# Gated linear attention and a SoLU block: v and state in 64 columns, and query products dealt out among the wide ones

## The chip, the cores and the metric

The kernel runs on one core of a Trainium2 chip. A core has a matrix engine (TensorE, PE in the profile; its weight loads are PEld), three engines for elementwise work (VectorE or DVE, ScalarE or ACT, GpSimd or POOL) and SyncE (SP), which issues most transfers. Each engine works through its own queue in order, and semaphores hold an instruction until what it needs is there. Products are written to PSUM, eight banks of 512 float32 columns on 128 partitions. The metric is device time in microseconds; the kernel before has a median of 407.49 over 14 runs (402.58 to 410.55).

## The reference

Attention with a decaying state for 4 batches, 8 heads, 768 tokens and 48 dimensions per head, then a feed-forward block on 3072 tokens (384 to 1024 to 384):

```python
for t in range(S):
    state = alpha[:, :, t, :, None] * state + np.einsum('bhd,bhe->bhde', k[:, :, t], v[:, :, t])
    y[:, :, t] = np.einsum('bhd,bhde->bhe', q[:, :, t], state)
# x = y as (tokens, heads * dims)
h = x @ w_in
e = np.exp(h - h_max)
solu = h * e / (sum(e) + 1e-09)
ln = (solu - mean(solu)) / sqrt(var(solu) + 1e-06) * g_ln
return ln @ w_out
```

All inputs and outputs are float32.

## The kernel before

Tokens are taken in six groups of 128 per batch; a group holds all four batches. Within a group attention is written as matrix products: running products of alpha scale queries and keys (`scan_back`, `scan_on`, `queries`, `keys`), `scores` multiplies keys with queries, `masked` keeps the causal half as `sT`, and the output `y` of a batch is the sum of two kinds of products, both made by `y_mm` (L298) into one PSUM bank per batch:

- `read_state` (L315): queries times the state left by the earlier groups. A head's 48 dimensions are split into 32 and 16. The 32 of head h lie in row h of `qv` and `state`; the 16 of two heads share a row of 32 partitions, and `qv` rows 8 to 15 hold that row once for each head, with the other head's half set to zero by `parity` (`apart`, L235). A product has 32 rows by 32 columns of weights and 128 tokens, so 16 of them have places of their own in the 128x128 array (four batches by four column places `r`). There are four parts: `parts` 0 and 1 give the first 32 output dimensions of heads 0 to 3 and 4 to 7, parts 2 and 3 the last 16 of the even and of the odd heads. Each part has 2 x 4 x 4 = 32 products, 128 in all.
- `read_values` (L323): `sT` times v, 64 products with all 128 rows and 32 columns of weights. Then ScalarE copies each batch's bank to `x`.

`next_state` (L333) makes keys times v: 32 products with 64 columns for the heads' first 32 key dimensions, 16 with 128 columns (two heads side by side) for the shared rows; VectorE adds the two banks to `state` (L351; in group 0 ScalarE copies them). `decay` (L246), on GpSimd, multiplies the state by the group's whole decay before it is read. `keys_back` (L284) turns the keys back with 12 transposes for `next_state`.

In `vn` and `state` a head has 80 columns: dimensions 0 to 31 in columns 0 to 31, dimensions 32 to 47 in 48 to 63, zeros elsewhere. `last` picks 32 columns that hold the 16 and 16 zeros, so the 16 of an even and of an odd head land on different halves of 32 output rows.

The feed-forward block has two wide products: `up_mm` (L362), three of 512 columns into `h`, and `down` (L471), four of 385 columns into `o` for each half. The program is written under a manual schedule: the order of calls is the order on each engine. For each group g the loop from L858 has eight steps s. A step makes `up(g, s)`, attention work of group g + 1, and half a `down` of group g - 1. Three tables, `first` (g = 1), `second` (g = 2) and `usual`, say which attention work stands at the head of a step, behind `up`, in the middle (ahead of `down`) and in the tail. So attention of group 2 stands in `first`, of group 3 in `second`, of groups 4 and 5 in `usual`; groups 0 and 1 stand in an opening written by hand (L651 to L783). In the steps that the change touches, `usual` has scores in the tails of steps 4 and 5, the masks at the heads of 5 and 6, query products of parts 0 and 1 in the tail of step 6, parts 2 and 3 in the middle of step 7, values and the next state in its tail. No group follows group 5.

The other queues that the change passes: SyncE issues the loads in the order of the program (`load_v`, two transfers a group, ahead of the loads of k and q of the next group), and GpSimd has the decay between running sums (L397) and the small `pow` instructions of `finish` (L508).

Of the kernel before, what the change touches and what calls it, by code (L numbers as in the profile page):

```python
# [9 lines left out]
FP = mybir.dt.float32  # L10
# [4 lines left out]
ALU = mybir.AluOpType  # L15
AX = mybir.AxisListType
P = 128
# [15 lines left out]
def fast_path(ctx, tc, q, k, v, alpha, moe_w_in, moe_w_out, moe_g_ln, out):  # L33
# [12 lines left out]
    nc = tc.nc  # L46
    B, H, S, D = q.shape
# [4 lines left out]
    NP = H // 2  # L52
    NB = H + NP
    E0, E1 = 32, 16
    KC = DM // P
    FC = DFF // P
    HF = FC // 2
# [7 lines left out]
    const = pool("const", 1)  # L65
# [37 lines left out]

    VW = 80
    vn = const.tile([P, B, H, VW], FP, name="vn")
    state = const.tile([P, 2 * H, VW], FP, name="state")
    last = [slice(48, 80), slice(32, 64)]
    SW = P + 1  # L110
    aT = const.tile([P, NB, SW], FP, name="aT")
    seed = [const.tile([P, NP, SW], FP, name=f"seed{i}") for i in range(2)]
# [53 lines left out]

    def load_v(g):
        t = slice(g * P, (g + 1) * P)
        for dst, src in ((slice(0, E0), slice(0, E0)), (slice(48, 64), slice(E0, D))):
            nc.sync.dma_start(  # L170
                out=vn[:, :, :, dst].rearrange("p b h d -> p (b h) d"),
                in_=v[:, :, t, src].rearrange("b h p d -> p (b h) d"),
            )

    def load_v_first(slot):
        x = slots[slot].rearrange("p (n d) -> p n d", d=D)
        y = vn.rearrange("p b h d -> p (b h) d")
        nc.sync.dma_start(out=x, in_=v[:, :, 0:P].rearrange("b h p d -> p (b h) d"))
        for dst, src in ((slice(0, E0), slice(0, E0)), (slice(48, 64), slice(E0, D))):
            nc.gpsimd.tensor_copy(out=y[:, :, dst], in_=x[:, :, src])  # L180


    def firsts(src, dst):
# [62 lines left out]
    def decay(g):  # L246

        if g == 0:
            return
        s = state[:, 0:H, 0:64]  # L250
        nc.gpsimd.tensor_tensor(out=s, in0=s, in1=h4[:, 0:H, 1:2].to_broadcast([P, H, 64]), op=ALU.mult)
        for i in range(2):
            s = state[:, H : 2 * H, 0:64].rearrange("p (j i) e -> p j i e", i=2)[:, :, i]
            nc.gpsimd.tensor_tensor(out=s, in0=s, in1=h4[:, H:NB, 1:2].to_broadcast([P, NP, 64]), op=ALU.mult)

    def quarter(b):
        return slice(32 * b, 32 * b + 32)

    def banks(name, shape, n=B):
        return [ps_a.tile([P] + shape, FP, tag=f"a{b}", name=f"{name}{b}") for b in range(n)]  # L260
# [30 lines left out]

    parts = [(a, [(NP * a + r, slice(0, E0)) for r in range(NP)]) for a in range(2)]
    parts += [(2, [(2 * r + i, last[i]) for r in range(NP)]) for i in range(2)]
    reading = {}

    def y_mm(b, a, r, row, lhsT, rhs, stop=False):  # L298
        begun = reading["begun"]
        nc.tensor.matmul(  # L300
            y_bank(b)[quarter(r), a], lhsT=lhsT, rhs=rhs, start=(b, r) not in begun, stop=stop,
            tile_position=(row, 32 * r), skip_group_check=True,
        )
        begun.add((b, r))

    def read_begin():
        reading["y"] = {}
        reading["begun"] = set()

    def y_bank(b):  # L310
        if b not in reading["y"]:
# [2 lines left out]

    def read_state(n):  # L315
        a, hs = parts[n]
        for rows in (0, H):
            for r, (h, e) in enumerate(hs):
                for b in range(B):
                    p = quarter(b)  # L320
                    y_mm(b, a, r, 32 * b, state[p, rows + h, e], qv[p, rows + h])

    def read_values(g, batches=range(B)):  # L323
        if 0 in batches:
            gr[g]["x"] = pair.tile([P, KC, B, P], FP, name="x")
        for b in batches:
            for n, (a, hs) in enumerate(parts):
                for r, (h, e) in enumerate(hs):
                    y_mm(b, a, r, 0, vn[:, b, h, e], sT[:, b, h], n == len(parts) - 1)
        for b in batches:  # L330
            nc.scalar.copy(out=gr[g]["x"][:, :, b], in_=reading["y"][b])  # L331

    def next_state(g):  # L333
        kv = banks("kv", [H, 64], 2)
        for j in range(NB):
            for b in range(B):
                if j < H:
                    o, e = kv[0][quarter(b), j], vn[:, b, j, 0:64]
                else:
                    i = 2 * (j - H)  # L340
                    o, e = kv[1][quarter(b), i : i + 2], vn[:, b, i : i + 2, 0:64]
                nc.tensor.matmul(  # L342
                    o, lhsT=kg[:, j, quarter(b)], rhs=e, start=True, stop=True, tile_position=(0, 32 * b),
                    skip_group_check=True,
                )
        for i in range(2):
            s = state[:, H * i : H * i + H, 0:64]
            if g == 0:
                nc.scalar.copy(out=s, in_=kv[i])
            else:  # L350
                nc.vector.tensor_tensor(out=s, in0=s, in1=kv[i], op=ALU.add)  # L351

# [7 lines left out]
    def up_mm(g, f):  # L362
        d = gr[g]
        h = ps_h.tile([P, T4], FP, tag="h", name="h")
        for a in range(KC):
            nc.tensor.matmul(  # L366
                h, lhsT=w_in[:, a, f * P : (f + 1) * P], rhs=d["x"][:, a].rearrange("p b t -> p (b t)"),
                start=(a == 0), stop=(a == KC - 1),
            )
        d["h"] = h  # L370

    def up_act(g, f):
# [95 lines left out]
        d["r"] = small.tile([P, B], FP, name="r4")  # L468
        nc.gpsimd.tensor_tensor(out=d["r"], in0=s[:, :, 3], in1=mhalf.to_broadcast([P, B]), op=ALU.pow)

    def down(n, half):  # L471
        g, b = divmod(n, B)
        d = st[n]
        if half == 0:
            d["o"] = ps_o.tile([P, 512], FP, tag="o", name="o")
        for f in range(half * HF, half * HF + HF):
            nc.tensor.matmul(  # L477
                d["o"][:, 0 : DM + 1], lhsT=u_of(g, f)[:, b * P : b * P + P], rhs=w_out[:, f], start=(f == 0),
                stop=(f == FC - 1), skip_group_check=True,
            )  # L480

    def finish(n):
        g, b = divmod(n, B)
# [143 lines left out]
    nc.scalar.dma_start(out=g_rows, in_=moe_g_ln.rearrange("(c p) -> c p", p=P))  # L627
    load_first(k, kn, 0)
    load_first(q, qn, 0)
    nc.gpsimd.memset(vn, 0.0)  # L630
    nc.gpsimd.memset(unit, 0.0)
    nc.gpsimd.memset(unit[:, :, 0:1], 1.0)
    nc.gpsimd.memset(aT[:, :, 0:1], 0.0)
# [42 lines left out]
    scores(0, 0)  # L676
    t = [x.tile([P, NP, P], FP, tag=n, name="a_" + n) for x, n in ((ps_h, "h"), (ps_o, "o")) for _ in range(2)]
    scores(0, 1, t)
    read_begin()
    masked(0)  # L680
    masked(1)
    bits(0)
# [7 lines left out]
    for f in range(FC):  # L690
        p = 2 + f // 2
# [75 lines left out]
    masked(1)  # L767
    finish(2)
    alpha_T(2)
    down(3, 0)  # L770
    read_begin()
    read_state(0)
    read_state(1)
    down(3, 1)
    read_state(2)
    read_state(3)
    alpha_over(2)
    load(alpha, an, 3)
    for i in range(3):
# [7 lines left out]
    usual = dict(  # L787
        head={4: "keys_back", 5: "masked0", 6: "masked1"},
        behind={0: "v keys", 1: "on2 on0 on1", 2: "lasts firsts", 3: "apart", 5: "decay", 6: "alpha", 7: "back"},
        tail={4: "scores0", 5: "scores1", 6: "begin read0 read1", 7: "values"},  # L790
        middle={7: "read2 read3"},
    )
    first = dict(
        head={4: "keys_back", 6: "masked0", 7: "masked1"},
        behind={0: "v keys", 1: "on2 on0", 2: "on1 lasts", 3: "firsts", 4: "apart", 5: "decay", 7: "alpha"},
        tail={5: "scores0", 6: "scores1", 7: "begin read0 read1 read2 read3 values"},
        middle={},
    )
    second = dict(
        head={4: "keys_back", 6: "masked0", 7: "masked1"},  # L800
        behind={0: "back_late", 1: "v keys", 2: "on2 on0 on1", 3: "lasts firsts", 4: "apart", 5: "decay", 6: "alpha", 7: "back"},
        tail={5: "scores0", 6: "scores1", 7: "read2 read3 values"},
        middle={7: "begin read0 read1"},
    )

    def attend(a, what):

        more = a + 1 < G
        if what == "v":
            load_v(a)  # L810
        elif what == "keys":
            keys_T(a)
            keys(a)
            if more:
                load(k, kn, a + 1)
        elif what[:2] == "on":
            scan_on(a, int(what[2]))
        elif what == "lasts":
            lasts(qn, qe)
            queries(2)  # L820
        elif what == "firsts":
            firsts(qn, qv[:, 0:H])
            queries(0)
            queries(1)
            if more:
                load(q, qn, a + 1)
        elif what == "apart":
            apart()
        elif what == "decay":
            decay(a)  # L830
        elif what == "keys_back":
            keys_back(a)
        elif what[:6] == "scores":
            scores(a, int(what[6]))
        elif what[:6] == "masked":
            masked(int(what[6]))
        elif what == "alpha" and more:
            alpha_T(a + 1)
            alpha_over(a + 1)
            if a + 2 < G:  # L840
                load(alpha, an, a + 2)
        elif what == "back" and more:
            for i in range(3):
                scan_back(a + 1, i)
        elif what == "back_late":
            for i in range(3):
                scan_back(a, i)
        elif what == "begin":
            read_begin()
        elif what[:4] == "read":  # L850
            read_state(int(what[4]))
        elif what == "values":
            read_values(a)
            next_state(a)

    centres = {4: (0, 1), 6: (2, 3), 7: (4, 5, 6, 7)}
    todo = []
# [528 lines left out]
```

## Time and profile before

| what | value |
|---|---|
| median of the runs | 407.49 us |
| the profiled execution | 403.4 us |
| its span, first to last instruction | 401.6 us |
| granted TensorE clock | 0.994 |
| TensorE products, busy | 375.2 us |
| VectorE busy | 255.8 us |
| ScalarE busy | 146.3 us |
| GpSimd busy | 117.6 us |
| `h`, 288 passes | 133.9 us |
| `o`, 384 passes | 133.2 us |
| queries with state, 1280 passes | 20.1 us |
| `sT` with v, 768 passes | 22.9 us |
| keys with v, 384 and 192 passes | 7.0 and 6.5 us |

A float32 product leaves two records on TensorE, called passes here; a transpose leaves one. In a row of the timeline the columns are the start and length in us, the engine, the line, the operation, output and inputs by name, the tile of the array (rows * columns of weights), the shape of the moving operand, the count, and in brackets the idle time before it with what ended it. Products overlap, so a group's busy time is the union of its records, and the step from one row's start to the next is what the row cost.

### The profile page before, as it was taken

The numbers are of one execution on the slowest core, as the hardware profiler recorded it, in microseconds if no ns is written. First come the engines' busy times: TensorE is split into PE (matmuls) and PEld (weight loads), VectorE is DVE, ScalarE is ACT, GpSimd is POOL, SyncE is SP. The second block draws the span as 40 slices with busy tenths as digits, with TensorE's granted clock in tenths as the row PEclk, the third lists the DMA queues.
The fourth block names the chain that finished last, engine by engine and source line by source line (L and its number), as shares of the span: only waits on it lengthen the run. The fifth ranks groups of instructions, "written<-read, shape, count | busy, mean of one in ns | idle before, by whom it ended". The sixth has DMA issues, their size and how long they took to land. (4 is left out here: it accounts for less than half of the span.)

```text
span 401.6 us, 11119 instructions
## 1 busy us (share of the span) xinstructions
PE 375.2 (93%) x4929; PEld 227.8 (57%) x4929; DVE 255.8 (64%) x415; ACT 146.3 (36%) x253; POOL 117.6 (29%) x118
## 2 busy tenths in 40 slices
PE   8686999779897998999999999999999999999995
PEld 8673355446653467555657555666556575555552
DVE  0979779996649883798691894674875413444510
ACT  3636674553432534223443143243152132233100
POOL 5010000030005894076510446210475110333200
PEclk9999999999999899999999999999999999999999
DMA  9966989304327304543040932003300000000011
GB/s 183 197 162 181 223 258 155 81 20 99 101 52 128 80 4 95 67 100 78 22 101 11 155 81 54 2 23 61 40 20 21 23 3 21 20 20 12 30 41 47
DMA packets 86410, 30.82 MB, mean 77 GB/s; under 512 B 67913, under 2 KB 84561, under 8 KB 86353
## 3 DMA queue, kind: packets, MB, share of 16 engines
q1 hardware_dynamic: 85328, 29.11, 33.6%
q8 instruction: 40, 0.66, 0.7%
q10 hardware_dynamic: 1024, 0.92, 0.7%
q14 instruction: 18, 0.14, 0.1%
HBM read 25.30 MB, written 4.72 MB: 75 GB/s over the span
## 5 line engine op out<-in xcount | busy, mean ns | idle before, releaser
L366 PE MATMUL h<-x,w_in 128*128 128x512 f32 x288 | 133.9, 606 | 6.3 <-ACT sq L559 3.7
L477 PE MATMUL o<-w_out,room 128*128 128x385 f32 x384 | 133.2, 491 | 1.1 <-DVE least L223 1.1
L477 PEld LDWEIGHTS o<-w_out,room 128*128 128x128 f32 x384 | 71.5, 190 | 57.0 <-issue 15.0
L366 PEld LDWEIGHTS h<-x,w_in 128*128 128x128 f32 x288 | 53.4, 192 | 66.5 <-issue 50.2
L381 DVE TENSOR_TENSOR room<-h,e 128x512 f32<-128x512 f32 x40 | 27.6, 690 | 56.7 <-ACT e L380 56.6
L508 POOL TENSOR_TENSOR r<-sums,mhalf 128x1 f32<-128x1 f32 x20 | 12.1, 606 | 168.9 <-DVE sums L500 168.8
L380 ACT ACTIVATE e<-h 128x512 f32<-128x512 f32 x40 | 23.9, 597 | 82.1 <-PE h L366 82.1
L397 POOL TENSOR_TENSOR p<-p,e 128x512 f32<-128x512 f32 x30 | 42.1, 1403 | 21.9 <-ACT e L380 21.7
L382 ACT ACTIVATE u<-room 128x512 f32<-128x512 f32 x40 | 25.2, 630 | 50.2 <-DVE room L381 50.2
L279 DVE TENSOR_TENSOR sT<-a,mask 128x512 f32<-128x512 f32 x44 | 27.3, 680 | 10.8 <-PE a L268 10.8
L268 PE MATMUL a<-qv,kT 32*128 32x128 f32 x704 | 24.6, 279 | 4.6 <-DVE qv L758 2.0
L268 PEld LDWEIGHTS a<-qv,kT 32*128 32x128 f32 x704 | 21.8, 186 | 11.6 <-issue 3.1
L397 DVE TENSOR_TENSOR p<-p,u 128x512 f32<-128x512 f32 x30 | 23.9, 798 | 7.0 <-ACT u L382 7.0
L209 DVE TENSOR_TENSOR_SCAN hT<-aT,unit 128x516 f32<-128x516 f32 x18 | 21.8, 1260 | 8.3 <-ACT aT L655 8.2
L209 DVE TENSOR_TENSOR_SCAN aT<-aT,seed 128x516 f32<-128x516 f32 x18 | 25.0, 1387 | 0.6
L351 DVE TENSOR_TENSOR state<-state,kv 128x512 f32<-128x512 f32 x10 | 6.9, 687 | 28.3 <-PE kv L342 28.3
L300 PE MATMUL y<-sT,vn 128*32 128x128 f32 x768 | 22.9, 274 | 1.7 <-issue 1.1
L300 PEld LDWEIGHTS y<-sT,vn 128*32 128x32 f32 x768 | 20.8, 110 | 4.1 <-issue 3.1
L331 ACT COPY x<-y 128x384 f32<-128x384 f32 x24 | 11.5, 480 | 31.6 <-PE y L300 31.6
L233 POOL TENSOR_TENSOR kT<-kT,hT 128x1024 f32<-128x1024 f32 (+1 forms) x8 | 13.7, 1739 | 31.3 <-DVE kT L184 31.3
L300 PE MATMUL y<-qv,state 32*32 32x128 f32 x1280 | 20.1, 278 | 1.7 <-issue 1.3
L300 PEld LDWEIGHTS y<-qv,state 32*32 32x32 f32 x1280 | 15.9, 103 | 9.2 <-issue 6.2
(140 smaller groups left out, 388.1 us busy)
## 6 DMA issues: line engine op xcount, KB each, us to landing
an<-in_alpha_dram SPq DMA_DIRECT2D x20, 192.0 KB, 4.4
out_dram<-o_sb SPq DMA_DIRECT2D x20, 192.0 KB, 1.9
room<-in_moe_w_out_dram SPq DMA_DIRECT2D x8, 384.0 KB, 4.8
kn<-in_k_dram SPq DMA_DIRECT2D x16, 192.0 KB, 4.3
qn<-in_q_dram SPq DMA_DIRECT2D x16, 192.0 KB, 3.5
vn<-in_v_dram SPq DMA_DIRECT2D x5, 512.0 KB, 5.7
room<-in_moe_w_in_dram SPq DMA_DIRECT2D x16, 128.0 KB, 3.8
kn<-in_k_dram SPq DMA_DIRECT2D x4, 384.0 KB, 5.8
```

Of the source, the lines that this page charges most:

```text
L209: nc.vector.tensor_tensor_scan(out=o, data0=a, data1=s, initial=1.0, op0=ALU.mult, op1=ALU.add)
L233: nc.gpsimd.tensor_tensor(out=kT[:, part], in0=kT[:, part], in1=hk[:, part], op=ALU.mult)
L268: nc.tensor.matmul(a[b][:, i], lhsT=kT[quarter(b), kb], rhs=qv[quarter(b), qb], start=kb == h, stop=kb != h, tile_position=(32 * b, 0), sk ...
L279: nc.vector.tensor_tensor(out=sT[:, b, half * NP : half * NP + NP], in0=a[b], in1=mask[:, None, :].to_broadcast([P, NP, P]), op=ALU.mult,)
L300: nc.tensor.matmul(y_bank(b)[quarter(r), a], lhsT=lhsT, rhs=rhs, start=(b, r) not in begun, stop=stop, tile_position=(row, 32 * r), skip_g ...
L366: nc.tensor.matmul(h, lhsT=w_in[:, a, f * P : (f + 1) * P], rhs=d["x"][:, a].rearrange("p b t -> p (b t)"), start=(a == 0), stop=(a == KC ...
L380: nc.scalar.activation(out=e, in_=h, func=AF.Exp)
L381: nc.vector.tensor_tensor(out=u, in0=h, in1=e, op=ALU.mult)
L382: nc.scalar.activation(out=u2, in_=u, func=AF.Square)
L397: eng.tensor_tensor(out=p, in0=d[0][i] if f == 1 else p, in1=d[f][i], op=ALU.add)
L477: nc.tensor.matmul(d["o"][:, 0 : DM + 1], lhsT=u_of(g, f)[:, b * P : b * P + P], rhs=w_out[:, f], start=(f == 0), stop=(f == FC - 1), skip ...
L508: nc.gpsimd.tensor_tensor(out=r, in0=s[:, 3:4], in1=mhalf, op=ALU.pow)
```

## The change

Four things:

1. A head has 64 columns in `vn` and `state`, 48 of them used. An even head has its dimensions in columns 0 to 47, an odd one has its first 32 in 32 to 63 and its last 16 in 16 to 31 (`first_of`, `last_of`, `all_of`). `load_v` has four transfers for two, the first load four copies for two, `next_state` has 48 and 96 columns for 64 and 128 and four additions for two, and `decay` has four multiplications of 192 elements for one of 512 and two of 256.
2. `ends_state` holds, for a shared row, the last 16 dimensions of both heads, each with the other head's rows of the state set to zero (block-diagonal); `decay` makes it with two more instructions. One set of 16 products with `qe` takes the place of two sets with the two halves of `qv`, so a group has 112 query products for 128.
3. Group 5 has no `keys_back` and no `next_state`.
4. `read_begin` makes the list of the query products. `deal` takes the next `pace` of them and stands after each wide product of `up_mm` and of `down`; what is left over is issued at the start of `read_values`. The pace is 10 in `usual`, from the middle of step 6; 16 in `second`, from the middle of step 7, and in group 1 from the fourth product of `down(3, 0)`; in `first` all 112 stand ahead of the values.

```diff
-    VW = 80
-    vn = const.tile([P, B, H, VW], FP, name="vn")
+    VW = 64
+    vt = const.tile([P, B * H * VW + 32], FP, name="vn")
+    vn = vt[:, 0 : B * H * VW].rearrange("p (b h d) -> p b h d", b=B, h=H)
     state = const.tile([P, 2 * H, VW], FP, name="state")
-    last = [slice(48, 80), slice(32, 64)]
+    ends_state = const.tile([P, NP, 2, E1], FP, name="ends_state")
+    all_of = [slice(0, D), slice(E1, VW)]
+    first_of = [slice(0, E0), slice(E0, 2 * E0)]
+    last_of = [slice(E0, E0 + E1), slice(E1, E0)]
+    last = [slice(E0, 2 * E0), slice(0, E0)]
...
     def load_v(g):
...
+        for dst, src in ((first_of, slice(0, E0)), (last_of, slice(E0, D))):
+            for i in range(2):
+                nc.sync.dma_start(
+                    out=vn.rearrange("p b (h i) d -> p i (b h) d", i=2)[:, i, :, dst[i]],
+                    in_=v[:, i::2, t, src].rearrange("b h p d -> p (b h) d"),
+                )
...
     def decay(g):
...
-        s = state[:, 0:H, 0:64]
-        nc.gpsimd.tensor_tensor(out=s, in0=s, in1=h4[:, 0:H, 1:2].to_broadcast([P, H, 64]), op=ALU.mult)
         for i in range(2):
-            s = state[:, H : 2 * H, 0:64].rearrange("p (j i) e -> p j i e", i=2)[:, :, i]
-            nc.gpsimd.tensor_tensor(out=s, in0=s, in1=h4[:, H:NB, 1:2].to_broadcast([P, NP, 64]), op=ALU.mult)
+            for rows, d in ((0, h4[:, i:H:2, 1:2]), (H, h4[:, H:NB, 1:2])):
+                s = state[:, rows + i : rows + H : 2, all_of[i]]
+                nc.gpsimd.tensor_tensor(out=s, in0=s, in1=d.to_broadcast([P, NP, D]), op=ALU.mult)
+            nc.gpsimd.tensor_scalar(
+                out=ends_state[:, :, i], in0=state[:, H + i : 2 * H : 2, last_of[i]], scalar1=parity[:, i : i + 1],
+                scalar2=None, op0=ALU.mult,
+            )
...
-    def read_begin():
+    def read_begin(pace):
         reading["y"] = {}
         reading["begun"] = set()
+        reading["left"] = [x for n in range(len(parts)) for x in read_state(n)]
+        reading["pace"] = pace
+
+    def deal(n=None):
+        left = reading.get("left", [])
+        for x in left[:n]:
+            y_mm(*x)
+        del left[:n]
...
     def read_state(n):
         a, hs = parts[n]
+        out = []
         for rows in (0, H):
+            if rows and n == 3:
+                break
             for r, (h, e) in enumerate(hs):
                 for b in range(B):
                     p = quarter(b)
-                    y_mm(b, a, r, 32 * b, state[p, rows + h, e], qv[p, rows + h])
+                    if rows and n == 2:
+                        s, q = ends_state[p, r].rearrange("p i d -> p (i d)"), qe[p, r]
+                    else:
+                        s, q = state[p, rows + h, e], qv[p, rows + h]
+                    out.append((b, a, r, 32 * b, s, q))
+        return out
 
     def read_values(g, batches=range(B)):
+        deal()
...
     def next_state(g):
-        kv = banks("kv", [H, 64], 2)
+        kv = banks("kv", [H, D], 2)
...
     def up_mm(g, f):
...
                 start=(a == 0), stop=(a == KC - 1),
             )
+            deal(reading.get("pace"))
...
-    def down(n, half):
+    def down(n, half, late=0):
...
+            if f >= half * HF + late:
+                deal(reading.get("pace"))
...
-    down(3, 0)
-    read_begin()
-    read_state(0)
-    read_state(1)
+    read_begin(16)
+    down(3, 0, 3)
     down(3, 1)
-    read_state(2)
-    read_state(3)
...
     usual = dict(
...
-        tail={4: "scores0", 5: "scores1", 6: "begin read0 read1", 7: "values"},
-        middle={7: "read2 read3"},
+        tail={4: "scores0", 5: "scores1", 7: "values"},
+        middle={6: "begin10"},
     )
     first = dict(
...
-        tail={5: "scores0", 6: "scores1", 7: "begin read0 read1 read2 read3 values"},
+        tail={5: "scores0", 6: "scores1", 7: "begin0 values"},
         middle={},
     )
     second = dict(
...
-        tail={5: "scores0", 6: "scores1", 7: "read2 read3 values"},
-        middle={7: "begin read0 read1"},
+        tail={5: "scores0", 6: "scores1", 7: "values"},
+        middle={7: "begin16"},
     )
...
-        elif what == "keys_back":
+        elif what == "keys_back" and more:
             keys_back(a)
...
         elif what == "values":
             read_values(a)
-            next_state(a)
+            if more:
+                next_state(a)
```

More of the change, by code (lines that the diff above doesn't have):

```diff
@@ L168, in load_v @@
         t = slice(g * P, (g + 1) * P)
[L169 to L173, printed above, removed]
+        for dst, src in ((first_of, slice(0, E0)), (last_of, slice(E0, D))):
[4 more added lines that the diff above has]
+                )
     def load_v_first(slot):
@@ L177, in load_v_first @@
         y = vn.rearrange("p b h d -> p (b h) d")
+        xi, yi = (z.rearrange("p (n i) d -> p i n d", i=2) for z in (x, y))
         nc.sync.dma_start(out=x, in_=v[:, :, 0:P].rearrange("b h p d -> p (b h) d"))
-        for dst, src in ((slice(0, E0), slice(0, E0)), (slice(48, 64), slice(E0, D))):
-            nc.gpsimd.tensor_copy(out=y[:, :, dst], in_=x[:, :, src])
+        for dst, src in ((first_of, slice(0, E0)), (last_of, slice(E0, D))):
+            for i in range(2):
+                nc.gpsimd.tensor_copy(out=yi[:, i, :, dst[i]], in_=xi[:, i, :, src])
     def firsts(src, dst):
@@ L289, in keys_back @@
             nc.scalar.copy(out=kg[:, NP * i : NP * i + NP], in_=t[i])
-    parts = [(a, [(NP * a + r, slice(0, E0)) for r in range(NP)]) for a in range(2)]
+    parts = [(a, [(NP * a + r, first_of[r % 2]) for r in range(NP)]) for a in range(2)]
     parts += [(2, [(2 * r + i, last[i]) for r in range(NP)]) for i in range(2)]
@@ L337, in next_state @@
                 if j < H:
-                    o, e = kv[0][quarter(b), j], vn[:, b, j, 0:64]
+                    o, e = kv[0][quarter(b), j], vn[:, b, j, all_of[j % 2]]
                 else:
                     i = 2 * (j - H)
-                    o, e = kv[1][quarter(b), i : i + 2], vn[:, b, i : i + 2, 0:64]
+                    at = (b * H + i) * VW
+                    e = vt[:, at : at + 160].rearrange("p (i d) -> p i d", i=2)[:, :, 0:D]
+                    o = kv[1][quarter(b), i : i + 2]
                 nc.tensor.matmul(
@@ L345, in next_state @@
                 )
[L346 to L351, printed above, removed]
+        for n in range(2):
+            for i in range(2):
+                s, x = state[:, H * n + i : H * n + H : 2, all_of[i]], kv[n][:, i::2]
+                if g == 0:
+                    nc.scalar.copy(out=s, in_=x)
+                else:
+                    nc.vector.tensor_tensor(out=s, in0=s, in1=x, op=ALU.add)
     def u_of(g, f):
@@ L629, in fast_path @@
     load_first(q, qn, 0)
-    nc.gpsimd.memset(vn, 0.0)
+    nc.gpsimd.memset(vt, 0.0)
     nc.gpsimd.memset(unit, 0.0)
@@ L678, in fast_path @@
     scores(0, 1, t)
-    read_begin()
+    read_begin(0)
+    reading["left"] = []
     masked(0)
@@ L769, in fast_path @@
     alpha_T(2)
-    down(3, 0)
-    read_begin()
-    read_state(0)
-    read_state(1)
+    read_begin(16)
+    down(3, 0, 3)
     down(3, 1)
-    read_state(2)
-    read_state(3)
     alpha_over(2)
@@ L847, in attend @@
                 scan_back(a, i)
[L848 to L851, printed above, removed]
+        elif what[:5] == "begin":
+            read_begin(int(what[5:]))
         elif what == "values":
             read_values(a)
-            next_state(a)
+            if more:
+                next_state(a)
     centres = {4: (0, 1), 6: (2, 3), 7: (4, 5, 6, 7)}
```

## The prediction

> **What bounds the kernel now.** I read the page first, then TensorE's timeline, then single instructions at the seams.
>
> ```profile
> PE 375.2 (93%) x4929; PEld 227.8 (57%) x4929; DVE 255.8 (64%) x415; ACT 146.3 (36%) x253; POOL 117.6 (29%) x118
> ```
>
> TensorE is busy for 93% of the span; in the stretches from 217 to 275 and 275 to 332 us the busy time per stretch is 58.0 of 58.0 and 57.0 of 57.0 us. A busy TensorE can still be badly fed, so the next view is its order of work. Columns: start, length, engine and line, operation, count (a float32 product leaves two records, "passes").
>
> ```profile
> 280.75 2.74 PE L366 MATMUL h<-x,w_in 128*128 128x512 f32 x6
> 283.33 2.76 PE L477 MATMUL o<-w_out,room 128*128 128x385 f32 x8
> 285.93 2.74 PE L366 MATMUL h<-x,w_in 128*128 128x512 f32 x6
> ...
> 296.26 1.47 PE L287 MATMUL tp<-ident,kT 128*128 128x128 f32 x12
> 297.57 2.74 PE L366 MATMUL h<-x,w_in 128*128 128x512 f32 x6
> ...
> 317.55 1.91 PE L300 MATMUL y<-qv,state 32*32 32x128 f32 x128
> 319.39 2.84 PE L366 MATMUL h<-x,w_in 128*128 128x512 f32 x6
> 322.16 1.91 PE L300 MATMUL y<-qv,state 32*32 32x128 f32 x128
> 324.00 2.86 PE L477 MATMUL o<-w_out,room 128*128 128x385 f32 x8
> 326.79 3.70 PE L300 MATMUL y<-sT,vn 128*32 128x128 f32 x128
> 330.30 1.95 PE L342 MATMUL kv<-vn,kg 128*32 128x64 f32 x96
> 332.18 2.84 PE L366 MATMUL h<-x,w_in 128*128 128x512 f32 x6
> ```
>
> Compare starts, not lengths. Between wide neighbours an `h` step takes 2.58 us and an `o` step 2.60. Between two blocks of 32x32 products the `h` step takes 2.77 and the `o` step 2.79: each is 0.19 longer. Single instructions show where that goes.
>
> ```profile
> L366 PE MATMUL h<-x,w_in x6: 593/593/697, 261.9 to 264.2; 128*128 128x512 f32 x6
> ```
>
> The first wide pass after small ones takes 697 ns, the other five 593: its weight load is exposed, 0.10 us. At the other end:
>
> ```profile
> 264.16 0.59 PE L366 MATMUL h<-x,w_in 128*128 128x512 f32 x1
> 264.68 0.58 PE L300 MATMUL y<-qv,state 32*32 32x128 f32 x33
> ```
>
> A wide pass streams for 2.58/6 = 0.43 us, so the one at 264.16 has streamed by 264.59, and the first small one starts at 264.68: 0.09 us. On the way back the last small pass starts at 261.71, streams 128 columns (0.43/4 = 0.107) and the wide one starts at 261.91: again 0.09. **A round trip from wide to small and back costs 0.09 + 0.09 + 0.10 = 0.28 us**, apart from the small products' own time. The second line also tells their own time: the 32 passes of the first 16 products all start within 0.33 us, so 16 products straight after a wide one take 0.34 us to the end of their stream. The block's other 48 take 1.84 - 0.09 - 0.32 = 1.43 us, 0.48 per 16.
>
> **The change, part by part.** All times are on TensorE unless named.
>
> *Dealing in the two usual groups (4 and 5).* Before, `o`, 64, `h`, 64, `o`, values: 326.79 - 314.87 = 11.92 us. After, ten products follow each of 11 wide ones, the last two stand before the values. Ten products take 0.34 - 6 x 0.0066 = 0.30 us (first passes start 6.6 ns apart); with the round trip 0.58. Ten batches: 5.8; the eleventh with the two left over and one change to the values' mode 0.09 + 0.31 + 0.09 = 0.5; wide streams 2.58 + 2.57 + 2.58 = 7.73. Sum 14.0, so +2.1 each, **+4.2 for two**. The 16 fewer products (112 for 128) are in it. The batch of ten is not in this trace; ends 0.25 us (two passes of 0.107 and ten starts of a few ns) and 0.51 (ten at the 0.030 us of the block's later products, plus two pass lengths). I take 0.30, since every batch stands straight behind a wide product, as the row's first 16 do.
>
> Two rules of the Trainium skill bear on this. "TensorEngine Tiling (Array Packing)", Key Properties, says that changing the tiling mode drains the engine; it has no price, and speaks against dealing: the rows price it at 0.18 us a round trip, 20 extra trips or so being 3.6 us. "TensorE: Matmul & The Clock Gate", Step-by-step: what each phase is for, says weight loads are pulled ahead of running matmuls; then the 0.10 us would hide, and the two groups would lose 2.2 rather than 4.2. The 697 ns pass says it does not hide across a change of mode, so I keep 4.2.
>
> *Group 3 (16 each, from the last step's `o`).* Here the trace has a wait:
>
> ```profile
> 152.71 0.41 PE L300 MATMUL y<-qv,state 32*32 32x128 f32 x4 [1.28 <-issue]
> ...
> 205.42 1.85 PE L300 MATMUL y<-qv,state 32*32 32x128 f32 x122 [0.20 <-DVE sT L279]
> 207.20 2.86 PE L477 MATMUL o<-w_out,room 128*128 128x385 f32 x8
> ```
>
> The block began at 204.10 and ended at 207.20, 3.10 us for 1.84, because the `y` banks were still being read by the masks on VectorE until 205.36. After, one `o` product (0.65) fills part of that wait. Walking it through: `o` 204.0 to 204.65, batch held until 205.42, done 205.75; then three `o` products with two batches of 16 at 0.34 + 0.28, and the last 64: values at 211.1 instead of 211.82, **-0.7**. *Group 2* deals nothing: 16 products fewer at 0.028, **-0.4**. *Group 1*: four batches at 0.62 and a block of 48 for two blocks of 64: 4.0 against 4.0, **0**.
>
> *Narrower state products.* From 330.30 to 332.18 less 0.09: 1.79 us for 32 products of 64 and 16 of 128 columns, four side by side, 2048 column passes, 0.87 ns each, near the wide products' 0.43/512 = 0.84. They stream, so 48 and 96 columns save a quarter, **-0.43 in groups 1 to 4, -1.7**; group 0 lies in the opening, where VectorE's weight repair shares the bound: -0.2. Ends 0 (another limit below 64 columns) and -0.45; I take near the full quarter, because the row sits at the stream's rate.
>
> *Nothing of the last group.* The transposes of keys go: 297.57 - 296.26 = **-1.3**. The state products go too, but they covered the copy of `x`:
>
> ```profile
> 330.55 0.48 ACT L331 COPY x<-y 128x384 f32<-128x384 f32 x1 [0.39 <-PE y L300]
> ```
>
> The fourth copy ends at 331.03, so `h` can start at 331.1 rather than 332.18: **-1.1**, not -1.88.
>
> *Off the path.* The decay on GpSimd: 1057 and 621 ns for 512 and 256 elements give 1.7 ns an element and 0.19 fixed; four of 192 and two of 64 are 2.6 us for 2.3, ended near 306.7, while the queries now start at 315.5 (2.0 earlier): 8 us of cover. Masks there end at 314.76, 0.7 us before the first dealt product needs a bank; were that cover gone, the batch would wait as in group 3. State additions: four of about 0.35 us for two of 0.69; queued behind them are the next group's small statistics, needed 5 us later. The v load has four transfers for two, the same bytes; SyncE waits for two more slots before the k load, but v landed in 5.7 to 7.5 us and is needed some 50 later, and k's load waits for VectorE anyway. First v: four copies of 0.61, 0.61, 0.38, 0.38 for 1.64, ending at 22.5 for products that start at 23.5 behind VectorE. Copies of group 0's state, four for two on ScalarE, are needed 48 us later.
>
> **Sum:** +4.2 - 0.7 - 0.4 + 0 - 1.7 - 0.2 - 1.3 - 1.1 = -1.2 us. The profiled execution took 403.4 us (span 401.6 and 1.8 around it), so 402.2, a ratio of 0.997; on the median of 407.49 that is **406.3 us**.
>
> **Rivals.** *Slower: the batches run at the later cadence.* Products 17 to 64 of a block already take 0.48 per 16; if a dealt ten starts like those, it takes 0.51 for 0.30. With 22 batches that is +4.6, so +3.4: 410.9. For it: between two batches only 0.65 us of wide work stands, where the row's first 16 followed 2.6 us. Against: 0.65 us is still more than twice the batch's own time. It decides from +0.15 us a batch (3.3 us over the sum, past +0.5%).
>
> *Faster: the stalls that the trace calls issue go away.* Rows at 108.81, 113.09 and 152.71 show TensorE idle for 1.14, 0.90 and 1.28 us inside long runs of small products, with nothing that the profile names. Shorter runs would end them: -3.3 more, 402.9. For it: 256 `y` passes stood before the one at 152.71; against: group 2 still runs 112 + 64 + 48 products in a row, and group 1 still 48 + 64 + 48. *Faster: loads hide.* By the rule above -2 more: 404.3. *The narrower products save nothing:* +0.7 in all, 408.2.
>
> **Chances.** The sum as worked, within 0.5% (about 2 us, what a measurement of this kernel can tell from no change): 0.46, its own range 404.5 to 408.5, the narrow products' failure included. Later cadence, or another wait at a dealt batch: 0.26. Stalls gone 0.18 and loads hidden 0.10: 0.28. Range from below the stalls' case to the later cadence's: 401.5 to 411.5.
>
> **What would show it.** `h` and `o` products between dealt batches as rows of two passes with the first 0.10 longer; dealt ten from start to next wide start about 0.39; groups 4 and 5 longer by 2 us from scores to values; the state row at 1.45 us; no `tp` in the last group and a wait for the copy ahead of its first `h`. Wrong if a dealt batch takes over 0.5, or if `issue` rows vanish or multiply.

## The result

The changed kernel is slower: 411.05 us median (406.14 to 415.23), 406.44 for the kernel before in the same comparison, ratio 1.0123 with a 95% interval of 1.008 to 1.0166. A second comparison of the same program, on another occasion, gave 1.0082 (1.0052 to 1.0112). The forecast was 406.3 us and no change. Ratios are of the fast executions alone; of the profiles below only that of the kernel with 32 small products is of a slower one (406.23 us, granted clock 0.983).

The page of the changed kernel, busy time by engine:

```profile
PE 377.3 (92%) x4661; PEld 218.2 (53%) x4661; DVE 253.6 (62%) x421; ACT 144.7 (35%) x252; POOL 121.9 (30%) x135
```

268 product records fewer than before, and yet 2 us more busy time in a span of 409.4 us. Its timeline of TensorE in group 5, which answers to the rows from 317.55 to 332.18 shown of before (start, length, line, what, count, idle time before it):

```profile
321.54 0.81 PE L513 MATMUL o<-w_out,room 128*128 128x385 f32 x2
322.28 0.46 PE L314 MATMUL y<-qv,state 32*32 32x128 f32 x20
322.67 0.91 PE L513 MATMUL o<-w_out,room 128*128 128x385 f32 x2
323.51 0.46 PE L314 MATMUL y<-qv,state 32*32 32x128 f32 x20
...
326.38 1.12 PE L401 MATMUL h<-x,w_in 128*128 128x512 f32 x2
327.43 0.46 PE L314 MATMUL y<-qv,state 32*32 32x128 f32 x20
...
335.67 3.70 PE L314 MATMUL y<-sT,vn 128*32 128x128 f32 x128
339.97 2.84 PE L401 MATMUL h<-x,w_in 128*128 128x512 f32 x6 [0.60 <-ACT x L363]
```

From the start of a dealt ten to the next wide product is 0.39 us, and a wide `o` product takes 0.84 for its 0.645 of streaming: a batch costs 0.58, as worked out. From `o` to the values it is 335.67 - 321.54 = 14.13 us where it was 11.92. The last `h` waits 0.60 us for the copy of `x`, with no state products ahead of it.

So this part went as forecast. What did not lies earlier. The same view, groups 1 to 3, rows that were held up:

```profile
113.62 2.06 PE L314 MATMUL y<-sT,vn 128*32 128x128 f32 x67 [1.34 <-issue]
...
117.35 0.95 PE L376 MATMUL kv<-vn,kg 128*32 128x48 f32 x38 [0.96 <-issue]
...
154.99 0.30 PE L314 MATMUL y<-qv,state 32*32 32x128 f32 x2 [1.17 <-issue]
155.00 0.39 PE L314 MATMUL y<-qe,ends_state 32*32 32x128 f32 x14
155.12 0.27 PE L314 MATMUL y<-qv,state 32*32 32x128 f32 x2
155.13 0.58 PE L314 MATMUL y<-qe,ends_state 32*32 32x128 f32 x17
155.44 0.39 PE L314 MATMUL y<-qv,state 32*32 32x128 f32 x7
155.55 0.27 PE L314 MATMUL y<-qe,ends_state 32*32 32x128 f32 x1
155.56 0.56 PE L314 MATMUL y<-qv,state 32*32 32x128 f32 x25
156.04 1.94 PE L314 MATMUL y<-sT,vn 128*32 128x128 f32 x60
158.72 2.05 PE L314 MATMUL y<-sT,vn 128*32 128x128 f32 x66 [0.73 <-issue]
160.50 0.30 PE L376 MATMUL kv<-vn,kg 128*32 128x48 f32 x6
160.60 0.28 PE L314 MATMUL y<-sT,vn 128*32 128x128 f32 x2
160.63 0.86 PE L376 MATMUL kv<-vn,kg 128*32 128x48 f32 x54
163.54 0.94 PE L376 MATMUL kv<-vn,kg 128*32 128x48 f32 x36 [2.05 <-issue]
...
223.13 0.36 PE L376 MATMUL kv<-vn,kg 128*32 128x96 f32 x4 [0.91 <-issue]
```

With a seventh of 0.31 at 216.23 they make 7.5 us; before there were three, 3.3 us. All stand in long runs of small products. The rows between the three gaps of group 2 can be counted: 128 passes from 154.99 to 158.72, and 128 again from there to 163.54. Each pass has a weight load beside it, so 256 instructions lie between one gap and the next.

A ruler for the rest: the stretch from the first wide product of one group of the loop to that of the next, which I call loops 1 to 4 (loop 1 holds the attention of group 2, loop 4 that of group 5).

| us | opening | loop 1 | loop 2 | loop 3 | loop 4 | tail |
|---|---|---|---|---|---|---|
| before | 114.65 | 43.89 | 58.68 | 57.48 | 57.48 | 69.42 |
| changed | 118.23 | 46.18 | 59.01 | 59.27 | 57.28 | 69.39 |
| changed, second profile | 112.06 | 46.46 | 59.04 | 59.26 | 57.28 | 69.39 |
| forecast difference | -0.6 | -0.8 | -1.1 | +1.7 | -0.3 | 0 |

Loops 3 and 4 were forecast to 0.1 us. Loops 1 and 2 missed by 3.1 and 1.4 us, 4.5 in all; their issue gaps grew from 1.28 to 5.17, 3.9 of it. The opening differs by 6 us between two profiles of one program.

### The profile page after: what moved, and what is told of

It reads as the page before. It is cut to its first block, busy times and chain, and to the rows that moved or that the text cites. A ratio compares the mean times of both kernels' runs of the same rounds, so it can differ in the third digit from the quotient of the medians.

```text
span 409.4 us, 10615 instructions
## 1 busy us (share of the span) xinstructions
PE 377.3 (92%) x4661; PEld 218.2 (53%) x4661; DVE 253.6 (62%) x421; ACT 144.7 (35%) x252; POOL 121.9 (30%) x135
## 5 line engine op out<-in xcount | busy, mean ns | idle before, releaser
L401 PE MATMUL h<-x,w_in 128*128 128x512 f32 x288 | 135.9, 610 | 8.6 <-DVE g_col L634 4.5
L513 PE MATMUL o<-w_out,room 128*128 128x385 f32 x384 | 138.6, 498 | 1.1 <-DVE least L234 1.1
L513 PEld LDWEIGHTS o<-w_out,room 128*128 128x128 f32 x384 | 70.3, 190 | 56.6 <-issue 20.1
L282 PE MATMUL a<-qv,kT 32*128 32x128 f32 x704 | 25.6, 285 | 4.3 <-DVE sums L533 1.5
L386 DVE TENSOR_TENSOR state<-state,kv 128x192 f32<-128x192 f32 x16 | 4.9, 351 | 25.0 <-PE kv L376 25.0
L314 PE MATMUL y<-qv,state 32*32 32x128 f32 x960 | 19.2, 279 | 1.2 <-issue 1.2
L314 PEld LDWEIGHTS y<-qv,state 32*32 32x32 f32 x960 | 9.8, 103 | 18.5 <-issue 16.4
```

Of the source, the lines that this page charges most:

```text
L282: nc.tensor.matmul(a[b][:, i], lhsT=kT[quarter(b), kb], rhs=qv[quarter(b), qb], start=kb == h, stop=kb != h, tile_position=(32 * b, 0), sk ...
L314: nc.tensor.matmul(y_bank(b)[quarter(r), a], lhsT=lhsT, rhs=rhs, start=(b, r) not in begun, stop=stop, tile_position=(row, 32 * r), skip_g ...
L401: nc.tensor.matmul(h, lhsT=w_in[:, a, f * P : (f + 1) * P], rhs=d["x"][:, a].rearrange("p b t -> p (b t)"), start=(a == 0), stop=(a == KC ...
L513: nc.tensor.matmul(d["o"][:, 0 : DM + 1], lhsT=u_of(g, f)[:, b * P : b * P + P], rhs=w_out[:, f], start=(f == 0), stop=(f == FC - 1), skip ...
```

## The experiments

**Dealing taken out, and dealing alone.** Theory A: round trips between tile modes cost what the rows say, and runs of small products outpace the supply of TensorE's instructions. Rival B: the new layout is to blame.

```diff
# dealing out of the changed kernel
-        tail={4: "scores0", 5: "scores1", 7: "values"},
-        middle={6: "begin10"},
+        tail={4: "scores0", 5: "scores1", 6: "begin0 half", 7: "values"},
+        middle={7: "rest"},
...
-        middle={7: "begin16"},
+        middle={7: "begin0 half"},
...
+        elif what == "half":
+            deal(64)
+        elif what == "rest":
+            deal()
```

In group 1 two blocks likewise. The other kernel is the one before with `deal`, the same paces and places, 128 products, 80 columns and the full last group.

> The changed kernel with the query products back in two blocks (64 and 48) at their old places; narrow v and state, the merged products and the shorter last group stay. Theory A (round trips of 0.28 us between tile modes, and runs of small products that outpace the supply of TensorE's instructions, which shows as idle time called issue): groups 4 and 5 shorter by 2.2 us each than in the changed kernel, group 3 by 1 to 2 as its dense run starts better supplied; 5 to 7 us faster than the changed kernel, ratio to the kernel before 0.990 to 0.998. Rival B (the narrow columns or the new v layout make it slow, not the dealing): it stays slower than before, ratio 1.007 or more.

> The kernel before with dealing alone: same paces and places, all 128 products, 80 columns, full last group. Theory A: round trips cost 2.2 us and a little in each of groups 4 and 5, and the dense runs of groups 1 to 3 stall as in the changed kernel or a little less: 4 to 8 us slower than before, ratio 1.010 to 1.020. Rival B: ratio 0.995 to 1.012, at most the two groups' round trips.

Undealt: 401.49 us, ratio 0.9922 (0.9892 to 0.9953), faster than before. Dealing alone: 413.23 us, 1.0201 (1.0132 to 1.027). The timeline of the undealt kernel, group 5:

```profile
314.84 1.90 PE L314 MATMUL y<-qv,state 32*32 32x128 f32 x128
316.67 2.84 PE L401 MATMUL h<-x,w_in 128*128 128x512 f32 x6
...
320.85 2.86 PE L513 MATMUL o<-w_out,room 128*128 128x385 f32 x8
323.64 3.70 PE L314 MATMUL y<-sT,vn 128*32 128x128 f32 x128
```

Loops 3 and 4 are 56.63 and 54.64 us: 2.64 less each than dealt, 0.85 and 2.84 less than before. Dealing alone makes both 60.22, 2.74 more than before. The undealt kernel had been expected to gain 2.2 a loop, not 2.64. B falls; narrow columns, merged products and the short last group together are a gain. But A was wrong on one thing: I expected undealt blocks to find a better supply in group 3, and loops 1 and 2 stayed at 46.14 and 58.88 us, with 6.7 us of issue gaps after 60 us. Dealing had not made the gaps; dealing alone has 4.0 us of them, for 3.3 before.

**Where a packet ends.** The page has a queue of instruction transfers (38 packets, 0.62 MB, so 16 KB each; 40 before). I take it for TensorE's: its 4661 passes and as many weight loads are 245 to a packet, near the 256 counted above. If a gap comes when a run reaches the end of what has been fetched, moving every later instruction by half a packet must move the gaps, though nothing else changes. Products that nobody reads, put where TensorE idles ahead of its first wide product, do that; each is four instructions.

```diff
+    pad = ps_o.tile([P, 512], FP, tag="o", name="pad")
+    for i in range(32):
+        nc.tensor.matmul(
+            pad[quarter(i % 4), 0:32], lhsT=ones[:, 0:32], rhs=ones[:, 0:32], start=True, stop=True,
+            tile_position=(0, 32 * (i % 4)), skip_group_check=True,
+        )
     for f in range(FC):
         p = 2 + f // 2
         up_mm(0, f)
```

> The changed kernel with 32 small products (32 columns, 128 instructions with their weight loads, half of one 16 KB instruction packet) in TensorE's idle time ahead of the first wide product, where it waits for w_in. They change nothing that is read later. Theory A: what counts is where a packet's end falls in a dense run, so the issue gaps of groups 1 to 3 (1.34, 0.96, 1.17, 0.73, 2.05, 0.31, 0.91, in all 7.5 us in the changed kernel) move and their sum changes by 1 us or more, either way; everything from group 4 on stays within 0.2 us. Rival C (the gaps come from data transfers at these places): same places, sum within 1 us.

> The same with 64 small products, 256 instructions, one whole packet: the phase of the packets is that of the changed kernel. Theory A: the issue gaps stand at the same instructions as in the changed kernel, their sum 6.5 to 8.5 us. Rival C: like the run with 32. In both runs the products keep TensorE from 2 to 4 us of idling ahead of the first wide product; if its granted clock holds there, the opening is 2 us shorter than in the profile of the changed kernel, where six wide passes took 5.26 us instead of 2.8.

With 32: 402.79 us, ratio 0.9961 (0.9931 to 0.9991). With 64: 407.17 us, 1.0071 (1.0035 to 1.0107). Timeline of the kernel with 32, the end of group 2's run:

```profile
154.27 0.41 PE L314 MATMUL y<-qv,state 32*32 32x128 f32 x4 [1.26 <-issue]
154.61 3.70 PE L314 MATMUL y<-sT,vn 128*32 128x128 f32 x128
158.12 1.52 PE L376 MATMUL kv<-vn,kg 128*32 128x48 f32 x96
```

and of the kernel with 64:

```profile
154.84 2.05 PE L314 MATMUL y<-sT,vn 128*32 128x128 f32 x66 [0.46 <-issue]
...
159.66 0.94 PE L376 MATMUL kv<-vn,kg 128*32 128x48 f32 x36 [2.05 <-issue]
...
218.94 0.36 PE L376 MATMUL kv<-vn,kg 128*32 128x96 f32 x4 [0.91 <-issue]
```

A whole packet leaves the gaps at the same products (`y` x66, `kv` x36, `kv` x4), two of them of the same 2.05 and 0.91 us as without, and only the one of 0.31 us is gone; half a packet removes those two, and 3.3 us of gaps are left for 7.5. Loop 1 falls to 42.96 us. One new gap of 0.35 us came in group 4 (loop 3: 59.89), so "everything from group 4 on within 0.2 us" did not hold. Rival C, data transfers in the way, falls with the places, which moved though the same data was loaded. And for the changed kernel's gap before 154.99 no data moves at all. The view of transfers from 152.5 to 155 us:

```profile
DMA packets 1, 0.02 MB, mean 7 GB/s; under 512 B 0, under 2 KB 0, under 8 KB 0
...
q8 instruction: 1, 0.02, 2.7%
```

That packet of instructions starts at 152.55 and has landed at 153.65; TensorE idles from 153.82 to 154.99. All the traces together say the same. The fourteen profiles hold 76 gaps of more than 0.15 us after 60 us. Each of them ends 1.2 to 1.6 us after a packet of instructions has landed. And counted over TensorE's passes and weight loads from the start of the program, all 76 stand 162 to 179 places past a multiple of 256. So a gap is a wait for the next 16 KB of instructions. What takes the 1.2 to 1.6 us after the landing is not shown.

My other expectation failed: the small products did not hold the clock in the opening. TensorE still idled for 3.35 us behind 32 of them and for 2.18 behind 64, and the six wide passes that followed took 5.46 and 4.51 us for 2.8 at full clock. Up to the end of group 0's state products it took 40.40 us with 32 (40.48 in the kernel with 32 and no dealing, below) and 39.00 with 64, for 40.72 and 36.68 in the two profiles without.

**Both gains, another pace, the kernel before moved by half a packet, and a repeat.**

```diff
# pace 16
-        middle={6: "begin10"},
+        middle={6: "begin16"},
```

> The changed kernel without dealing (blocks of 64 and 48 at the old places) and with the 32 small products ahead of the first wide one, which shift the instruction packets by half a packet. Theory A: the two gains add. Against the run without dealing the issue gaps fall from 7.3 us to 3 to 4.5 us, so 3 us faster than it, ratio to the kernel before 0.980 to 0.989. If the gaps are rather set by how dense the blocks are, undealt blocks keep them at 6 us or more and the ratio stays 0.989 to 0.996.

> The changed kernel with 16 query products after each wide one in groups 4 and 5, where it has 10: 7 batches for 11. Theory A (each batch pays a round trip of 0.28 us and 0.30 to 0.34 of its own): groups 4 and 5 take 1.7 to 2.1 us less each than with 10, and 0.6 to 1.0 more than as two blocks (56.63 and 54.64 us from one group's first wide product to the next one's in the run without dealing); groups 1 to 3 and their issue gaps as in the changed kernel. A rival in which the small products themselves run slower when dealt would leave the groups near the 59.27 and 57.28 us of pace 10.

> The kernel before with the same 32 small products ahead of its first wide product, and nothing else. Theory A: the kernel before owes its time to the place of its packets too: its issue gaps (1.14, 0.90 and 1.28 us at 108.8, 113.1 and 152.7) move, and their sum of 3.3 us changes by 1 us or more, either way; groups 4 and 5 stay at 57.5 us each. If the gaps depend on the changed code alone, sum within 0.5 us and a ratio of 0.997 to 1.003.

> The changed kernel once more, beside the others on one chip. Theory A: issue gaps to 0.1 us as in its first profile (2.05 and 0.91 us for the two in the state products), since nothing but the program's addresses sets them; time 4 to 6 us over the kernel before. What is left of the 7.8 us between the two first profiles after the gaps (4.1) and the round trips lies ahead of the first state products, where the granted clock fell: there this profile may differ from the first by 2 us or more.

Undealt and moved by half a packet: 395.05 us, ratio 0.9764 (0.9707 to 0.9822), better than the lower end expected for it. Its gaps are 0.75 and 1.30 us. Pace 16: 403.93 us, 1.0004 (0.9975 to 1.0033); loops 3 and 4 at 57.38 and 55.39, 1.9 less than pace 10 and 0.75 more than two blocks. Seven batches for eleven, at the prices of the prediction 7 x 0.62 for 11 x 0.58, are 2.0 us less: the price per batch is right. Its timeline:

```profile
313.83 0.50 PE L314 MATMUL y<-qv,state 32*32 32x128 f32 x32
314.26 0.91 PE L513 MATMUL o<-w_out,room 128*128 128x385 f32 x2
315.10 0.50 PE L314 MATMUL y<-qv,state 32*32 32x128 f32 x32
```

The kernel before, moved by half a packet: 409.46 us, ratio 1.0111 (1.0078 to 1.0144), slower by as much as the change made it. Its timeline of groups 2 and 3 has gaps at places where it had none:

```profile
149.98 1.10 PE L300 MATMUL y<-qv,state 32*32 32x128 f32 x68 [1.32 <-issue]
151.01 1.94 PE L300 MATMUL y<-sT,vn 128*32 128x128 f32 x60
153.43 2.05 PE L300 MATMUL y<-sT,vn 128*32 128x128 f32 x66 [0.48 <-issue]
...
158.81 1.18 PE L342 MATMUL kv<-vn,kg 128*32 128x64 f32 x36 [2.43 <-issue]
...
218.04 2.04 PE L300 MATMUL y<-sT,vn 128*32 128x128 f32 x65 [1.04 <-issue]
...
222.04 1.17 PE L342 MATMUL kv<-vn,kg 128*32 128x64 f32 x34 [1.07 <-issue]
```

The repeat gave 407.35 us and the second row of the ruler. Its gap sum is 7.4 us again, but not "to 0.1 us": the long one was 2.60 us where it had been 2.05, the last 0.91 both times. It was 3.3 us slower than the kernel before, where 4 to 6 had been expected.

**Two more places each.** Expected and measured for 16 and 48 small products:

> The changed kernel without dealing and with 16 small products ahead of the first wide one: a quarter of an instruction packet. Theory A: groups 4 and 5 at 56.6 and 54.6 us as without the small products; the issue gaps another sum between the 7.3 us of none and 2.1 us of 32, or up to 1 us outside; ratio to the kernel before 0.974 to 0.995, in the order of the gap sums.

> The same with 48, three quarters of a packet. Theory A: as with 16; the phase lies between those of 32 (2.1 us of gaps) and of a whole packet (7.3 us), ratio 0.974 to 0.995.

> The kernel before with 16 small products ahead of its first wide one. Theory A: groups 4 and 5 at 57.5 us; issue gaps between the 3.3 us of none and the 7.6 us of 32, or up to 1 us outside; ratio 0.995 to 1.015. Were the kernel before at its best place already, both this run and the next are slower than it.

> The kernel before with 48. Theory A: as with 16, ratio 0.995 to 1.015. Over four places each, the kernel without dealing is faster than the kernel before by 1.5 to 2.2%.

| kernel, small products ahead | issue gaps after 60 us | loop 1 | loop 2 | loop 3 | loop 4 | ratio to the kernel before |
|---|---|---|---|---|---|---|
| before, 0 | 3.3 | 43.89 | 58.68 | 57.48 | 57.48 | 1 |
| before, 16 | 5.0 | 46.08 | 60.53 | 57.71 | 57.48 | 1.0072 (1.0038 to 1.0107) |
| before, 48 | 5.5 | 46.22 | 60.09 | 57.48 | 57.48 | 1.0069 (1.0036 to 1.0102) |
| before, 32 | 7.1 | 47.24 | 63.23 | 57.48 | 57.48 | 1.0111 (1.0078 to 1.0144) |
| changed, 32 | 3.3 | 42.96 | 58.01 | 59.89 | 57.28 | 0.9961 (0.9931 to 0.9991) |
| changed, 64 | 6.6 | 46.09 | 58.70 | 59.26 | 57.28 | 1.0071 (1.0035 to 1.0107) |
| changed, 0 | 7.5 | 46.18 | 59.01 | 59.27 | 57.28 | 1.0123 (1.008 to 1.0166) |
| undealt, 32 | 2.1 | 42.96 | 57.23 | 56.84 | 54.64 | 0.9764 (0.9707 to 0.9822) |
| undealt, 16 | 4.0 | 43.89 | 59.06 | 57.50 | 54.65 | 0.9823 (0.9785 to 0.9861) |
| undealt, 48 | 5.6 | 46.35 | 59.09 | 56.63 | 54.64 | 0.9869 (0.9804 to 0.9934) |
| undealt, 0 | 6.7 | 46.14 | 58.88 | 56.63 | 54.64 | 0.9922 (0.9892 to 0.9953) |
| pace 16, 0 | 6.6 | 45.63 | 59.27 | 57.38 | 55.39 | 1.0004 (0.9975 to 1.0033) |
| dealing alone, 0 | 4.0 | 43.78 | 59.91 | 60.22 | 60.22 | 1.0201 (1.0132 to 1.027) |

Undealt with 16, loop 3 was expected at 56.6 us and took 57.50: a new gap of 0.52 stands in it. Within a kernel the ratio follows the sum of the gaps to within the intervals: undealt, 4.6 us of gaps and 1.6% (6.4 us) from end to end; the kernel before, 3.8 us of gaps and 1.1% (4.5 us). The gaps that can be seen are the larger part of it, not all. The kernel before stands at its best place of the four, the changed one at the worse of its two (64 is 0 over again). Over places 0 and 32, where both were run, the kernel before averages (1 + 1.0111)/2 = 1.0056, the changed one (1.0102, the mean of two, and 0.9961) 1.0032: 0.998 of it, where the sum of the prediction said 0.997; two places are few for such an average. Over all four places the undealt kernel is at 0.978 of the kernel before.

## Why the prediction was wrong

*Dealing, groups 4 and 5:* right. +2.1 us each; 14.13 - 11.92 = 2.21 measured. The batch of ten, which the trace of before did not have, took the 0.30 us chosen, and the rival of the later cadence did not happen. The skill's rule by which loads would hide under running products did not hold across modes: a wide `o` product between batches took 0.84 us for 0.645, which is the two changes of mode at 0.09 and the extra 0.1 us.

*Narrow state products:* right where they are fed. From 281.23 to 282.69 the row takes 1.46 us for 1.88, forecast 1.45. In groups 1 to 3 the gap sits in that very row, and the saving is swallowed.

*Last group:* right. Its `tp` is gone and the first `h` waits for the copy: -2.4 forecast for transposes and state products together; with +2.2 for dealing that makes -0.2, and loop 4 measured -0.20.

*Group 1:* right. From the `o` to the values it took 9.30 us for 9.27 (110.35 - 101.05 and 106.61 - 97.34), forecast 0.

*Group 3:* the -0.7 came true by luck.

```profile
209.90 0.81 PE L513 MATMUL o<-w_out,room 128*128 128x385 f32 x2
210.64 0.50 PE L314 MATMUL y<-qv,state 32*32 32x128 f32 x32
...
214.46 0.96 PE L314 MATMUL y<-qv,state 32*32 32x128 f32 x57
...
216.96 3.90 PE L314 MATMUL y<-sT,vn 128*32 128x128 f32 x126
```

The walk held the first batch for the masks until 1.42 us after the start of its `o` (204.0 to 205.42). It started after 0.74 us without a wait, since the masks had ended at 210.52. That won 0.68, and the block of 64 before the values lost as much: 216.96 - 214.46 = 2.50 us for 1.74 (1.83 for such a block before, less the change of mode). So `o` to values took 7.06 us, 0.66 less than before. Behind them lies the miss: from the values to the next `h` it is 6.46 us for 5.40, where the narrower state products were to save 0.43. Of this 0.91 is the gap in the state row. The loop was forecast at -1.1 and measured +0.33.

*The step that failed* is the one that has no line in the sum: the issue gaps. The prediction saw three of them, 3.3 us, and treated them as a property of long runs that could only shrink when runs are broken up ("Faster: the stalls that the trace calls issue go away"). The sum carried them over unchanged, and though "multiply" stood among the signs of being wrong, it had no price. They are a property of where 16 KB of instructions end, and fewer instructions ahead moved those ends. The count shows by how much: group 2's values stand behind 4279 passes and weight loads in the kernel before and behind 4151 in the changed one. The 16 query products that the merging saves in group 1 and the 16 in group 2 are 128 instructions, half a packet. Adding 32 small products brings the changed kernel back to 4279, and the gap is again at the last four query passes (1.26 us, 1.28 before). The kernel before with 32 small products has the changed kernel's three gaps of group 2 at the changed kernel's places: 68 query passes ahead of the values, and at the rows shown as `y` x66 and `kv` x36. In loops 1 and 2 they grew by 3.9 us, which turns a forecast of -1.2 into +2.7, and 1.0123 and 1.0082 are +5.0 and +3.3. What is left is not settled: 0.6 us in loops 1 and 2 without a visible gap, why some packet ends in a run have a gap and others none, and the opening, whose clock differs from one execution to the next. The rival on the slower side named another mechanism.

The Trainium skill has the mechanism, and I had not weighed it: "Runtime: NRT & Kernel Launch", Instruction fetch mechanics, says that an engine's instructions are refilled in 16 KiB blocks of 256 while it runs, and that this stays hidden because dispatch is slower than the refill. The block agrees with the trace (0.62 MB in 38 packets). Hidden it is not: a block of 64 query products is 256 instructions and takes 1.83 us, and the changed kernel's packets in group 3's run start at 213.6, 217.4, 220.7 and 224.3 us, 3.4 to 3.8 us apart.

## What to carry to other kernels

Rows of idle time called issue inside runs of small products, a multiple of 256 instructions apart, say that a kernel is short of instructions there. Then an edit upstream, even one that removes work, can move the time: 128 instructions that did nothing moved it by 1.1 to 1.6% here. Run each variant at two or more places of its instruction packets before its time is credited to the edit. Price a change of tile mode from the seams of the trace (here 0.28 us a round trip) and keep small products together unless a batch hides more than that. When work is taken away, look for what it had been covering: 1.88 us of state products were worth 1.1.

## What the runs showed of the hardware

An instruction gap nearly repeats: 2.05 us at the same product of three kernels (changed, changed with 64, undealt), though it was 2.60 in the repeat. The granted clock in the opening is not the same in two executions of one program. First profile of the changed kernel, then the second:

```profile
34.04 5.26 PE L401 MATMUL h<-x,w_in 128*128 128x512 f32 x6 [4.52 <-DVE g_col L634]
```

```profile
32.46 2.81 PE L401 MATMUL h<-x,w_in 128*128 128x512 f32 x6 [1.24 <-DVE g_col L634]
```

After 4.52 us of idling six wide passes took 5.26 us, with a granted clock of 0.58 from 34 to 40 us; after 1.24 us they took 2.81 at 1.00. The length of that idling does not decide it alone: the kernel before idled 3.67 us there and kept its clock (1.00), the changed one with 64 small products idled 2.18 and ran at 0.62. What decides is open.
